# Opening of a fused attention and mixer kernel: first matmul tile by tile, one weight half on another queue, banks of premade queries by count

## Chip, cores, metric

The kernel runs on one core of a Trainium2 chip. The metric is the device time of one execution in microseconds (us); the time before is the median of three runs.

## The reference, cut

x is 2048 tokens by 512, in bf16. All that matters here:

```python
xn = layernorm(x)
q = (xn @ wq)                       # 32 heads of 128
s = softmax(q k^T / sqrt(128)) v    # 2048 cached keys and values per head
s = s @ wo
h = gelu(layernorm(xn) @ w1)        # 512 -> 512
hs = shift(h) @ w2                  # each quarter of the columns shifted by 1 or 2 tokens
x1 = xn + hs
b = x1 + gelu(layernorm(x1) @ w3) @ w4
out = x + s * silu(b)
```

For layernorm(xn), a normalised row normalised again, the kernel uses xn itself. The change concerns xn, xn @ w1 and the first few xn @ wq.

## The kernel before, in words

Tokens come in 16 tiles of 128. The work has three parts: an opening (L466 to L498 and the lines behind it) that makes xn, its transpose xnT, the mixer's first matmul and the first queries; the rest of the mixer and the MLP (m2, x1, ln2, m3, m4); and a long loop over 128 attention units (group of four heads, quarter of the tokens, head), which fills almost all of the time and keeps TensorE at work with scores, weighted values and output products.

Every instruction is pinned in program order, so each engine's order is the order in which the Python code emits it. An instruction that waits holds all that stand behind it on its engine, a DMA's issue among them: SyncE (nc.sync) and ScalarE (nc.scalar) issue loads as instructions of their own queues. DMA semaphores are reused, so a later load can wait, before it is issued, for the landing of an earlier one.

The steps of the opening, per tile t: `ln1_stats` (L189, VectorE: two statistics instructions; GpSimd: two small ones for the inverse root, L175 and L176), `ln1_norm` (L192, VectorE, writes xall), `tr_pe` (L195: four TensorE transposes into a bank of the pool psO, then ScalarE copies them to xnT, L199). `m1(c0, w)` (L204) multiplies w1 with w columns of xnT, in two steps of eight matmuls, each into a two-bank tile of psS, each followed by a gelu on ScalarE (L213) into hT. `m2` (L217) multiplies hT with w2, `x1` (L224) adds it to xall on VectorE. Tiles 8 to 15 are transposed by DMA (`tr_dma`, L201) from SyncE's queue. `q_ahead` (L509) makes one query block ahead of the loop: four matmuls of 512 columns into a bank of psX ("xa" or "xm", one buffer each), then a copy by ScalarE (L277). `tr_q` (L514) is a `q_ahead` and a `tr_pe`.

Before the change the opening loads x tiles 0 to 3 on both queues, both halves of w1 on SyncE (L468, L469), four wq blocks on ScalarE (L471), then a junk gelu (L472) that brings in the activation table. Twelve matmuls on zeros (L477) keep TensorE at work until the first transposes. The first four tiles go through in pairs: stats 0 and 1, norm 0, transposes 0, stats 2, norm 1, transposes 1, `m1(0, 256)`, stats 3, norm 2, transposes 2, norm 3, transposes 3, `m1(256, 256)`. Later blocks of four tiles use `ln1_block` (L498), which starts each block with the stats of its first tile. Queries are made ahead in four batches of four; the last batch (2 * HG, NU - 12, NU - 2, NU - 1) is numbers 8, 116, 126 and 127.

Of the kernel before, what the change touches and what calls it, by code (L numbers as in the profile page):

```python
# [8 lines left out]
ACT = mybir.ActivationFunctionType  # L9
ALU = mybir.AluOpType  # L10
FP32 = mybir.dt.float32
# [6 lines left out]
def kernel(  # L18
# [15 lines left out]
    nc = tc.nc  # L34
    P = nc.NUM_PARTITIONS
# [4 lines left out]
    _, H, Sk, Dh = A_k_cache.shape  # L40
# [3 lines left out]
    NT = Sq // P  # L44
    QT = Sq // 512
    DC = D // P
# [4 lines left out]
    HG = 4  # L51
# [6 lines left out]
    BASE_J = [3, 3, 2, 2]  # L58
# [3 lines left out]
    pin = tc.keep_in_program_order  # L62

    def pool(name, bufs=1, space=None, **kw):
        if space is not None:
            kw["space"] = space
        return tc.tile_pool(name=name, bufs=bufs, **kw)
# [3 lines left out]
    xnT = const.tile([P, DC, Sq], BF16, name="xnT")  # L71
# [11 lines left out]
    warm = const.tile([P, 512], BF16, name="warm")  # L83
# [9 lines left out]
    psX = ent(pool("psX", 1, PSUM))  # L93
    mid = ExitStack()
    psS = mid.enter_context(pool("psS", 2, PSUM, reuse_waits="tile"))
# [8 lines left out]
    w1_v = B_w1.rearrange("(dc p) j -> p dc j", p=P)  # L104
# [3 lines left out]
    def mm(out, lhsT, rhs, start, stop):  # L108
        pin(nc.tensor.matmul(out=out, lhsT=lhsT, rhs=rhs, start=start, stop=stop))  # L109
# [8 lines left out]
        out=ident[:], in0=diag[:], scalar1=0.0, scalar2=None, op0=ALU.is_equal))  # L118
# [34 lines left out]
    def load_w(h, eng=nc.sync):  # L153
        wqs[h] = wqp.tile([P, DC, Dh], BF16, name="wq_h")
        pin(eng.dma_start(out=wqs[h][:], in_=wq_v[:, :, h * Dh:(h + 1) * Dh]))
# [3 lines left out]
    def load_x(t, eng):  # L159
        xin[t] = tokp.tile([P, D], BF16, tag="ta", bufs=10, name="xin")  # L160
        pin(eng.dma_start(out=xin[t][:], in_=xsrc[t]))
# [3 lines left out]
    w1_sb = pL.tile([P, DC, D], BF16, name="w1_sb")  # L165
    w2_sb = pL.tile([P, DC, D], BF16, name="w2_sb")
    w3_sb = [pL.tile([P, DC, 2 * P], BF16, name=f"w3_sb{i}") for i in range(FC // 2)]
    hT = pL.tile([P, DC, Sq + PADW], BF16, name="hT")
# [9 lines left out]
    def stats(src, mv, rs, t):  # L178
        bn = smp.tile([P, nc.vector.BN_STATS_DIM], FP32, name="bn")
        pin(nc.vector.bn_stats(out=bn[:], in_=src))  # L180
        pin(nc.vector.bn_aggr(out=mv[:, t, :], in_=bn[:]))
        rsqrt(rs[:, t:t + 1], mv[:, t, 1:2])

    def norm_to(out, src, mv, rs, t):
        pin(nc.vector.tensor_scalar(
            out=out, in0=src, scalar1=mv[:, t, 0:1], scalar2=rs[:, t:t + 1],
            op0=ALU.subtract, op1=ALU.mult))

    def ln1_stats(t):  # L189
        stats(xin[t][:], mv1, rs1, t)  # L190

    def ln1_norm(t):  # L192
        norm_to(xall[:, t, :], xin.pop(t)[:], mv1, rs1, t)

    def tr_pe(t):  # L195
        tp = psO.tile([P, DC, P], FP32, tag="ps_o", name="ps_o")
        for dc in range(DC):
            mm(tp[:, dc, :], xall[:, t, dc * P:(dc + 1) * P], ident[:], True, True)
        pin(nc.scalar.activation(out=xnT[:, :, t * P:(t + 1) * P], in_=tp[:], func=ACT.Identity))  # L199
# [4 lines left out]
    def m1(c0, w):  # L204
        for jp in range(DC // 2):
            b = BASE_J[2 * jp]
            ps = psS.tile([P, 2, 512], FP32, name="ps_s")
            for j in range(2):
                jc = 2 * jp + j
                for dc in range(DC):  # L210
                    mm(ps[:, j, 0:w], w1_sb[:, dc, jc * P:(jc + 1) * P],
                       xnT[:, dc, c0:c0 + w], dc == 0, dc == DC - 1)
            pin(nc.scalar.activation(  # L213
                out=hT[:, 2 * jp:2 * jp + 2, b + c0:b + c0 + w], in_=ps[:, :, 0:w],
                func=ACT.Gelu_apprx_tanh))

    def m2(t):  # L217
        ps = psO.tile([P, D], FP32, tag="ps_o", name="ps_o")
        for jc in range(DC):
            c0 = BASE_J[jc] + t * P - SHIFT[jc]  # L220
            mm(ps[:], hT[:, jc, c0:c0 + P], w2_sb[:, jc, :], jc == 0, jc == DC - 1)
        return ps
# [41 lines left out]
    def q_mm(u, dcs, tag="xa"):  # L264
        g, qt, hh = units[u]
        if dcs[0] == 0:
            st[u] = dict(psq=psX.tile([P, 512], FP32, tag=tag, name="ps_q"))
        for dc in dcs:
            mm(st[u]["psq"][:], wqs[g * HG + hh][:, dc, :],
               xnT[:, dc, qt * 512:(qt + 1) * 512], dc == 0, dc == DC - 1)  # L270

    def q_copy(u, eng=None):
        qT = qtp.tile([P, 512], BF16, name="qT")
        if eng is None:
            pin(nc.vector.tensor_copy(out=qT[:], in_=st[u].pop("psq")[:]))  # L275
        else:
            pin(nc.scalar.activation(out=qT[:], in_=st[u].pop("psq")[:], func=ACT.Identity))  # L277
        st[u]["qT"] = qT
# [187 lines left out]
    for t, eng in enumerate([nc.sync, nc.scalar, nc.sync, nc.scalar]):  # L466
        load_x(t, eng)
    pin(nc.sync.dma_start(out=w1_sb[:, 0:2, :], in_=w1_v[:, 0:2, :]))  # L468
    pin(nc.sync.dma_start(out=w1_sb[:, 2:4, :], in_=w1_v[:, 2:4, :]))  # L469
    for h in range(HG):  # L470
        load_w(h, nc.scalar)  # L471
    pin(nc.scalar.activation(out=junk[:], in_=ones_t[:], func=ACT.Gelu_apprx_tanh))  # L472
    for t in range(4, 8):
        load_x(t, nc.sync)
    pin(nc.sync.dma_start(out=w2_sb[:], in_=w2_v))
    wps = psX.tile([P, 512], FP32, tag="xm", name="ps_warm")
    for _ in range(12):  # L477
        mm(wps[:], warm[:, 0:P], warm[:], True, True)
    for jc in range(DC):
        b = BASE_J[jc]  # L480
        pin(nc.gpsimd.memset(hT[:, jc, 0:b], 0.0))
        pin(nc.gpsimd.memset(hT[:, jc, b + Sq: Sq + PADW], 0.0))

    ln1_stats(0)
    ln1_stats(1)
    ln1_norm(0)
    tr_pe(0)
    ln1_stats(2)
    ln1_norm(1)
    tr_pe(1)  # L490
    m1(0, 256)
    ln1_stats(3)
    ln1_norm(2)
    tr_pe(2)
    ln1_norm(3)
    tr_pe(3)
    m1(256, 256)
    def ln1_block(ts, tr):  # L498
        ln1_stats(ts[0])
        for a, b in zip(ts, ts[1:]):  # L500
            ln1_stats(b)
            ln1_norm(a)
            tr(a)
        ln1_norm(ts[-1])
        tr(ts[-1])

    made = []

    def q_ahead(u):  # L509
        q_mm(u, range(DC), ("xa", "xm")[u % 2])  # L510
        q_copy(u, nc.scalar)
        made.append(u)

    def tr_q(t):  # L514
        q_ahead(t - 4)
        tr_pe(t)

    for t in range(8, 16):
        load_x(t, nc.sync)
    ln1_block(range(4, 8), tr_q)  # L520
    pend = [(t, m2(t)) for t in range(2)]
    ln1_block(range(8, 12), tr_dma)
    m1(512, 512)
    for t, ps in pend:
        x1(t, ps)
    for u in range(HG, 2 * HG):
        q_ahead(u)
    pend = [(t, m2(t)) for t in range(2, 4)]
    ln1_block(range(12, 16), tr_dma)
    for h in range((NG - 1) * HG, NG * HG):  # L530
        wqs[h] = pL.tile([P, DC, Dh], BF16, name=f"wq_e{h}")
        pin(nc.sync.dma_start(out=wqs[h][:], in_=wq_v[:, :, h * Dh:(h + 1) * Dh]))
# [7 lines left out]
    for u in range(NU - 4 * HG, NU - 3 * HG):  # L540
        q_ahead(u)
# [57 lines left out]
    for g in range(NG - 1):  # L599
        b = (g * QT + QT - 1) * HG  # L600
        for hh in range(HG):
            h = (g + 1) * HG + hh
# [81 lines left out]
    for n in range(UB * SPU):  # L684
        u, p = divmod(n, SPU)
# [42 lines left out]
    n = UB * SPU  # L728
# [23 lines left out]
    def bank(pl, tag, **kw):  # L752
        return pl.tile([P, D], FP32, tag=tag, name="ps_w", **kw)[:]

    ps = {0: bank(psX, "xm")}
# [81 lines left out]
```

## Time and profile before

| | us |
|---|---|
| runs | 1260.08, 1260.21, 1258.32 |
| median | 1260.08 |
| profiled execution, its time | 1261.13 |
| profiled execution, its span | 1259.4 |

The profile is of one execution. Its page gives the busy time of each engine (PE is TensorE, PEld its weight loads, DVE VectorE, ACT ScalarE, POOL GpSimd, SP SyncE), the chain of work that ended last, and groups of instructions. The trace answers further views: instructions in order of time (start, duration, engine, line, tiles, count, and in brackets the idle time before and what ended it), where ACTq and SPq stand for the queues that issue DMAs; the chain in order of time; busy times of stretches; and DMA rates of a stretch, by queue (q1 is SyncE's, q10 ScalarE's). A tile's name is shortened: w_sb is w1, w2, w3 or w4, told apart by the line.

### The profile page before, as it was taken

How to read it: one execution, taken by the hardware profiler on the slowest of the kernel's cores; microseconds unless marked ns; L12 is line 12 of the kernel's file. 1: busy time of each engine (PE TensorE's matmuls, PEld its weight loads, DVE VectorE, ACT ScalarE, POOL GpSimd, SP SyncE). 2: the span in 40 equal slices, each digit the busy share in tenths (PEclk: the TensorE clock that was granted, in tenths of full speed). 3: DMA queues.
4: the chain of work that ended last, by engine and by line, in shares of the span. 5: the costliest groups of instructions: out<-in, count | busy, mean ns of one | idle time of the engine just before them, and what ended most of it. 6: DMA issues, size and time to landing. Idle time of an engine off the chain costs nothing.

```text
span 1259.4 us, 16202 instructions
## 1 busy us (share of the span) xinstructions
PE 1239.5 (98%) x5782; PEld 598.3 (48%) x5899; DVE 1033.0 (82%) x1430; ACT 1100.7 (87%) x1113; POOL 34.4 (3%) x91
## 2 busy tenths in 40 slices
PE   8999999999999999999999999999999999999997
PEld 4444444444444444444444444444444444444443
DVE  7621567788888988888898988988898999988888
ACT  4344889999998999999999999999999999898886
POOL 4320000000000000000000000000000000000000
PEclk9999999999999999999999999999999999999999
DMA  6492012444345423454354524553364434452222
GB/s 155 106 169 72 10 30 46 82 91 93 60 72 97 110 58 76 88 110 84 47 101 94 104 50 76 96 116 69 55 101 102 101 66 82 92 97 54 68 56 59
DMA packets 224945, 103.86 MB, mean 82 GB/s; under 512 B 176928, under 2 KB 208160, under 8 KB 224864
## 3 DMA queue, kind: packets, MB, share of 16 engines
q1 hardware_dynamic: 221648, 100.07, 40.9%
q0 software_dynamic: 672, 1.84, 0.8%
q8 instruction: 46, 0.75, 0.3%
q10 hardware_dynamic: 2544, 0.92, 0.3%
q14 instruction: 35, 0.29, 0.1%
HBM read 67.90 MB, written 2.36 MB: 56 GB/s over the span
## 4 chain that ended last, share of the span: by engine, by line
PE 88%; DMA 5%; DVE 5%; ACT 1%; issue 1%; DVEq 0%; ACTq 0%; SPq 0%
PE ps_s L109 36%; PE ps_o L109 33%; PE ps_q L109 8%; PE ps_wo L109 8%; DMA rb<-dr 3%; PE ps_m L109 2%; DMA dr<-rc 2%; DVE oT L358 1%; DVE acc L302 1%; DVE sacc L411 1%; DVE sm L338 1%; DMA tT<-acc 0%; PE ps_warm L109 0%; ACT pT L291 0%; ACT xnT L199 0%
## 5 line engine op out<-in xcount | busy, mean ns | idle before, releaser
L291 ACT ACTIVATE pT<-ps_s 128x1024 bf16<-128x1024 f32 x1024 | 1034.6, 1023 | 79.1 <-PE ps_s L109 31.4
L109 PE MATMUL ps_s<-qT,kT 128*128 128x512 bf16 x2041 | 607.5, 379 | 0.6
L109 PE MATMUL ps_o<-pT,vb 128*128 128x512 bf16 x1962 | 588.9, 379 | 2.3 <-DVE oT L358 1.8
L302 DVE TENSOR_TENSOR acc<-acc,pT 128x2048 bf16<-128x2048 bf16 x255 | 309.2, 1213 | 73.4 <-ACT pT L291 68.6
L109 PEld LDWEIGHTS <-kT 128*128 128x128 bf16 x2048 | 231.0, 113 | 226.2 <-issue 0.8
L109 PEld LDWEIGHTS <-vb 128*128 128x128 bf16 x2048 | 200.2, 98 | 228.3 <-issue 3.0
L109 PE MATMUL ps_wo<-wo_h,oT 128*128 128x512 bf16 x492 | 177.8, 379 | 2.1
L109 PE MATMUL ps_q<-xnT,wq_h 128*128 128x512 bf16 x481 | 172.7, 379 | 2.1
L297 DVE TENSOR_TENSOR acc<-pT 128x2048 bf16<-128x2048 bf16 x128 | 155.7, 1216 | 6.1 <-ACT pT L291 5.9
L358 DVE TENSOR_TENSOR oT<-ps_o,rb 128x512 bf16<-128x512 f32 x127 | 124.4, 980 | 30.5 <-DMA rb<-dr 29.7
L307 DVE TENSOR_TENSOR acc<-acc 128x1024 bf16<-128x1024 bf16 x127 | 87.9, 692 | 4.3
L275 DVE CAST qT<-ps_q 128x512 bf16<-128x512 f32 x112 | 76.5, 683 | 0.3 <-PE ps_q L109 0.3
L109 PEld LDWEIGHTS <-oT 128*128 128x128 bf16 x508 | 48.5, 98 | 56.6 <-DVE oT L358 1.1
L109 PEld LDWEIGHTS <-wq_h 128*128 128x128 bf16 x484 | 47.2, 98 | 56.2 <-issue 0.2
L411 DVE TENSOR_TENSOR sacc<-ps_wo,sacc 128x512 f32<-128x512 f32 x96 | 65.5, 683 | 3.2 <-PE ps_wo L109 2.7
L338 DVE TENSOR_REDUCE sm<-tT 128x4 f32<-128x512 bf16 x96 | 64.7, 674 | 1.8 <-DMA tT<-acc 1.8
L308 DVE TENSOR_TENSOR acc<-acc 128x512 bf16<-128x512 bf16 x127 | 54.0, 425 | 4.3
L242 ACT ACTIVATE h2T<-ps_s 128x1024 bf16<-128x1024 f32 x28 | 28.6, 1023 | 24.1 <-PE ps_s L109 24.1
L109 PE MATMUL ps_s<-xn2T,w_sb 128*128 128x512 bf16 x219 | 48.6, 379 | 0.3
L109 PEld LDWEIGHTS <-w_sb 128*128 128x128 bf16 x304 | 29.7, 98 | 34.6 <-issue 2.1
L109 PEld LDWEIGHTS <-h2T 128*128 128x128 bf16 x224 | 21.5, 98 | 25.0 <-issue 0.2
L109 PE MATMUL ps_m<-w_sb,h2T 128*128 128x512 bf16 x106 | 31.0, 379 | 0.5
(73 smaller groups left out, 333.5 us busy)
## 6 DMA issues: line engine op xcount, KB each, us to landing
rb<-dr SPq DMA_DIRECT2D x127, 256.0 KB, 4.2
vb<-in_A_v_cache_dram SPq DMA_DIRECT2D x64, 256.0 KB, 3.3
wo_h<-in_A_wo_dram SPq DMA_DIRECT2D x32, 128.0 KB, 3.6
wq_h<-in_A_wq_dram SPq DMA_DIRECT2D x28, 128.0 KB, 3.3
w_sb<-in_B_w_dram SPq DMA_DIRECT2D x9, 256.0 KB, 5.0
kT<-in_A_k_cache_dram SPq DMA_TRANSPOSE x128, 3.3
xl<-in_A_x_dram SPq DMA_DIRECT2D x16, 128.0 KB, 3.7
dr<-rc SPq DMA_DIRECT2D x127, 2.0 KB, 1.4
```

The lines of the kernel that those rows point to most:

```text
L109: pin(nc.tensor.matmul(out=out, lhsT=lhsT, rhs=rhs, start=start, stop=stop))
L242: pin(nc.scalar.activation(out=h2[c, f][:], in_=ps[:], func=ACT.Gelu_apprx_tanh))
L275: pin(nc.vector.tensor_copy(out=qT[:], in_=st[u].pop("psq")[:]))
L291: pin(nc.scalar.activation(out=s["pT"][-1][:, jj:jj + 2, :], in_=sps[:], func=ACT.Exp, scale=SCALE))
L297: pin(nc.vector.tensor_tensor(out=s["acc"][:], in0=s["pT"][0][:], in1=s["pT"][1][:], op=ALU.add))
L302: pin(nc.vector.tensor_tensor(out=a[:], in0=a[:], in1=st[u]["pT"][i][:], op=ALU.add))
L307: pin(nc.vector.tensor_tensor(out=a[:, 0:2, :], in0=a[:, 0:2, :], in1=a[:, 2:4, :], op=ALU.add))
L308: pin(nc.vector.tensor_tensor(out=a[:, 0, :], in0=a[:, 0, :], in1=a[:, 1, :], op=ALU.add))
L338: pin(nc.vector.tensor_reduce(out=sm[:], in_=s["tT"][:], axis=mybir.AxisListType.X, op=ALU.add))
L358: pin(nc.vector.tensor_tensor(out=to, in0=o, in1=rb, op=ALU.mult))
L411: pin(nc.vector.tensor_tensor(out=sa, in0=ps[:], in1=sa, op=ALU.add))
```

## The change

Loads: the second half of w1 goes to ScalarE's queue ahead of the wq blocks; the fourth wq block goes to SyncE's queue, behind x tiles 4 to 7 and ahead of w2. Warm matmuls: eleven ahead of the first transposes, one between those of tiles 0 and 1. Statistics: always one tile ahead of the norm, across blocks as well (`ln1` takes the place of `ln1_block`). First matmul of tiles 0 to 3: one tile at a time, 16 matmuls of 128 columns into a one-bank tile (two in psX, two in psS), between the transposes of later tiles; its gelus are two per tile, of 128x256. In ScalarE's order the copies of transposes 0, 1 and 2 come ahead of the gelus of tile 0. Banks: a premade query takes "xa" or "xm" by how many were made before it, not by its number.

```diff
-    pin(nc.sync.dma_start(out=w1_sb[:, 2:4, :], in_=w1_v[:, 2:4, :]))
-    for h in range(HG):
+    pin(nc.scalar.dma_start(out=w1_sb[:, 2:4, :], in_=w1_v[:, 2:4, :]))
+    for h in range(HG - 1):
         load_w(h, nc.scalar)
...
     for t in range(4, 8):
         load_x(t, nc.sync)
+    load_w(HG - 1)
...
-    for _ in range(12):
-        mm(wps[:], warm[:, 0:P], warm[:], True, True)
+    def warm_mm(n):
+        for _ in range(n):
+            mm(wps[:], warm[:, 0:P], warm[:], True, True)
+
+    warm_mm(11)
...
+    def ln1(t, tr):
+        if t + 1 < NT:
+            ln1_stats(t + 1)
+        ln1_norm(t)
+        tr(t)
+
+    def m1_tile(t, pl, tag):
+        ps = pl.tile([P, DC, P], FP32, tag=tag, name="ps_m1")
+        for jc in range(DC):
+            for dc in range(DC):
+                mm(ps[:, jc, :], w1_sb[:, dc, jc * P:(jc + 1) * P],
+                   xnT[:, dc, t * P:(t + 1) * P], dc == 0, dc == DC - 1)
+        return ps
+
+    def gelu_tile(t, ps):
+        for jp in range(DC // 2):
+            b = BASE_J[2 * jp] + t * P
+            pin(nc.scalar.activation(
+                out=hT[:, 2 * jp:2 * jp + 2, b:b + P], in_=ps[:, 2 * jp:2 * jp + 2, :],
+                func=ACT.Gelu_apprx_tanh))
+
     ln1_stats(0)
-    ln1_stats(1)
-    ln1_norm(0)
-    tr_pe(0)
-    ln1_stats(2)
-    ln1_norm(1)
-    tr_pe(1)
-    m1(0, 256)
-    ln1_stats(3)
-    ln1_norm(2)
-    tr_pe(2)
-    ln1_norm(3)
-    tr_pe(3)
-    m1(256, 256)
-    def ln1_block(ts, tr):
...
+    ln1(0, tr_pe)
+    warm_mm(1)
+    ln1(1, tr_pe)
+    pm = [m1_tile(0, psX, "xa")]
+    ln1(2, tr_pe)
+    gelu_tile(0, pm[0])
+    pm.append(m1_tile(1, psX, "xm"))
+    ln1(3, tr_pe)
+    gelu_tile(1, pm[1])
+    for t in (2, 3):
+        gelu_tile(t, m1_tile(t, psS, "ps_s"))
...
-        q_mm(u, range(DC), ("xa", "xm")[u % 2])
+        q_mm(u, range(DC), ("xa", "xm")[len(made) % 2])
...
-    ln1_block(range(4, 8), tr_q)
+    for t in range(4, 8):
+        ln1(t, tr_q)
...
-    ln1_block(range(8, 12), tr_dma)
+    for t in range(8, 12):
+        ln1(t, tr_dma)
...
-    ln1_block(range(12, 16), tr_dma)
+    for t in range(12, 16):
+        ln1(t, tr_dma)
```

More of the change, by code (lines that the diff above doesn't have):

```diff
@@ L482 @@
         pin(nc.gpsimd.memset(hT[:, jc, b + Sq: Sq + PADW], 0.0))
-    ln1_stats(0)
-    ln1_stats(1)
-    ln1_norm(0)
-    tr_pe(0)
-    ln1_stats(2)
-    ln1_norm(1)
-    tr_pe(1)
-    m1(0, 256)
-    ln1_stats(3)
-    ln1_norm(2)
-    tr_pe(2)
-    ln1_norm(3)
-    tr_pe(3)
-    m1(256, 256)
-    def ln1_block(ts, tr):
[L499 to L505, printed above, removed]
+    def ln1(t, tr):
[16 more added lines that the diff above has]
+                func=ACT.Gelu_apprx_tanh))
+    ln1_stats(0)
+    ln1(0, tr_pe)
[9 more added lines that the diff above has]
+        gelu_tile(t, m1_tile(t, psS, "ps_s"))
     made = []
     def q_ahead(u):
-        q_mm(u, range(DC), ("xa", "xm")[u % 2])
+        q_mm(u, range(DC), ("xa", "xm")[len(made) % 2])
         q_copy(u, nc.scalar)
```

## The prediction

> **What bounds the kernel now.** I read the page first: span, busy times, the chain that ended last.
>
> ```profile
> span 1259.4 us, 16202 instructions
> PE 1239.5 (98%) x5782; PEld 598.3 (48%) x5899; DVE 1033.0 (82%) x1430; ACT 1100.7 (87%) x1113; POOL 34.4 (3%) x91
> PE 88%; DMA 5%; DVE 5%; ACT 1%; issue 1%; DVEq 0%; ACTq 0%; SPq 0%
> ```
>
> TensorE is busy for 1239.5 of 1259.4 us, and no other engine is as full. So only the 20 us in which it stands still, and any matmul time that is added, can move the end. The profiled execution took 1261.13 us, 1.73 us more than its span; the median of the three runs is 1260.08, about 1.05 us below it. I work out a difference against the profiled span and subtract it from the median. 0.2% is 2.5 us here, about what a measurement can tell from no change.
>
> The view by stretches tells where TensorE stands still in the part that the diff touches. The columns are us in the stretch, then busy us of each engine.
>
> ```profile
> 8.00:14.00 6.00, 4.59 (x42) 3.90 (x43) 4.73 (x13) 3.21 (x7) 3.56 (x10) 1.00 1.03 295
> 20.00:45.00 25.00, 24.76 (x113) 11.04 (x115) 15.99 (x35) 10.81 (x14) 6.69 (x17) 1.00 0.64 148
> 45.00:51.00 6.00, 4.63 (x22) 1.94 (x21) 3.85 (x10) 2.29 (x4) 3.08 (x8) 1.00 0.29 25
> ```
>
> There are two holes: 1.4 us between 8 and 14, and 1.4 us between 45 and 51. Between them it is busy for 24.76 of 25 us, so time won in the first hole is carried through. The chain of waits, in order of time, says what the first hole is made of.
>
> ```profile
> 6.94 1.15 ACT xnT L199 x2
> 8.14 1.92 PE ps_s L109 x16
> 10.08 0.60 ACT hT L213
> 10.68 0.98 ACT xnT L199 x2
> 11.71 1.91 PE ps_s L109 x16
> ...
> 14.52 0.60 ACT qT L277
> 15.11 0.49 ACT xnT L199
> ```
>
> ScalarE copies two transposed tiles, TensorE multiplies the two, ScalarE has a gelu and two copies to do, TensorE waits. From 14.52 on ScalarE alternates query copies and tile copies without a gap, 0.60 + 0.49 us a turn, until the last xnT. So the opening's result is read off at one point: when does the first query copy start, 14.52 now?
>
> **The change, part by part. 1. The queues.** The second half of w1 goes from SyncE's queue to ScalarE's, ahead of the wq loads, and the fourth wq load goes to SyncE's. In the changed kernel's instruction order this leaves a wait that the old one doesn't have: the third wq load, issued by ScalarE, now waits for the first half of w1 to land (the semaphore it reuses). Before, the third and the fourth waited for xin tiles 1 and 3. Behind that load in ScalarE's own queue stand the table load, the junk gelu and every xnT copy. When does that half land?
>
> ```profile
> 1.64 0.43 SPq L468 DMA_DIRECT2D w_sb<-in_B_w_dram  x1
> 4.42 0.37 ACTq L155 DMA_DIRECT2D wq_h<-in_A_wq_dram  x1
> 4.82 1.28 ACT L472 ACT_TABLE_LOAD   x1 [4.82 <-DMA xin<-in_A_x_dram]
> 6.12 0.20 ACT L472 ACTIVATE junk<-ones_t 128x1 bf16<-128x1 bf16 x1
> 6.45 0.33 SPq L161 DMA_DIRECT2D xin<-in_A_x_dram  x1
> 8.24 0.43 SPq L475 DMA_DIRECT2D w_sb<-in_B_w_dram  x1
> ```
>
> The half is issued at 1.64. The 6.45 row is the load of xin tile 6, which in the old order waits for just this half: it lands at about 6.45, 4.8 us after its issue. From the release of the last ScalarE load (4.42) to the end of the junk gelu (6.32) are 1.90 us. So if the half lands at L, ScalarE is ready for the first xnT at R = L + 1.92, where before it was ready at 6.32 and waited for TensorE until 6.94. Does L stay at 6.45 when the other half shares the transfer engines from the start?
>
> ```profile
> DMA packets 1242, 0.63 MB, mean 286 GB/s; under 512 B 823, under 2 KB 1242, under 8 KB 1242
> q1 hardware_dynamic: 447, 0.43, 60.4%
> q10 hardware_dynamic: 795, 0.20, 40.1%
> DMA packets 792, 0.76 MB, mean 378 GB/s; under 512 B 54, under 2 KB 792, under 8 KB 792
> ```
>
> The first three rows are 4.2 to 6.4 us: 0.63 MB at 286 GB/s, with 823 packets under 512 B on it, those of wq. The last row is 10.6 to 12.6, where nearly all packets are larger: 378 GB/s. In the changed kernel both halves, 0.51 MB, follow the four x tiles, of which the last lands at 4.42 (ScalarE's release above). From 4.2 that is 1.8 us at the first rate and 1.4 at the second, so the data is there at 5.6 to 6.0, and something follows until the semaphore. From above, a landing as slow as the slowest row of this stretch (wq, 6.2 us after its issue) would give 7.85; from below, part of the first half has moved before 4.2, so 5.2. I take L = 6.2, near the row of the same transfer, and R = 8.12. On SyncE the fourth wq load now stands ahead of w2 and x tiles 8 to 15 and waits for the second half, which by the same rates lands at about L too. That is 2 us before w2 goes out now (8.24), so I cost this at nothing; if the cover were gone, w2 would be late for m2, after the four queries. [...]
>
> **2. Tiles one by one.** What does one tile's first matmul cost? No row has these 16 matmuls of 128 columns; the nearest are the transposes, which are the same size.
>
> ```profile
> 9.78 0.54 PEld L109 LDWEIGHTS <-xall 128*128 128x128 bf16 x8
> 9.88 0.61 PE L109 MATMUL ps_o<-ident,xall 128*128 128x128 bf16 x8
> L213 ACT ACTIVATE hT<-ps_s 128x512 bf16<-128x512 f32 x4 | 2.4, 599 | 2.8 <-PE ps_s L109 2.8
> L213 ACT ACTIVATE hT<-ps_s 128x1024 bf16<-128x1024 f32 x2 | 2.1, 1026 | 3.5 <-PE ps_s L109 3.5
> ```
>
> Eight weight loads take 0.54 us, the last of them 0.1, so a pair has 0.063 us and a tile 1.01. Four tiles are 4.04 us where the two calls of m1 now take 1.92 + 1.91 in the chain: 0.2 us more TensorE work, but in pieces that fit between the copies. The gelu of 128x256: the two rows give 0.43 us for 512 more columns, so 0.60 - 0.21 = 0.385, two per tile 0.77. Now the sum from R = 8.12, with 0.575 for an xnT copy (two in 1.15), 0.25 for four transposes, 0.2 until a result can be read and 0.04 from a copy to the matmul behind it:
> - xnT0 8.12 to 8.70, xnT1 to 9.27. TensorE: tile 0 8.74 to 9.75, transposes of tile 2 to 10.00, readable at 10.20.
> - ScalarE: xnT2 10.20 to 10.78, two gelus to 11.57. TensorE meanwhile: tile 1 10.00 to 11.01, transposes of tile 3 to 11.26.
> - ScalarE: xnT3 11.57 to 12.15, gelus of tile 1 to 12.92. TensorE: tile 2 11.26 to 12.27, tile 3 12.27 to 13.28, the first query 13.28 to 14.14, readable at 14.34.
> - ScalarE: gelus of tile 2 to 13.69, of tile 3 to 14.46, then the first query copy: 14.46 instead of 14.52.
>
> So the opening wins 0.06 us: the pieces overlap well, and the later start of ScalarE, 8.12 against 6.94, takes it back. In general the gain is 6.26 - L: -1.6 at 7.85, +1.06 at 5.2. Is VectorE in the way, with the statistics of the next tile ahead of each norm?
>
> ```profile
> 7.72 0.41 DVE L185 TENSOR_SCALAR xall<-xin,mv,rs 128x512 bf16<-128x512 bf16 x1
> 8.90 0.41 DVE L185 TENSOR_SCALAR xall<-xin,mv,rs 128x512 bf16<-128x512 bf16 x1 [0.77 <-POOL rs L176]
> ```
>
> The norms of tiles 2 and 3 stand at 7.72 and 8.90; the new order puts the statistics of tile 4 into the 0.77 us that the second one waits for GpSimd anyway, so it stays there, and the transposes want it only at 11.01: 1.7 us of cover, at the price of whatever is missing should xin tile 4 land after 9.7. It is issued earlier than now. The later norms come some 1 us earlier, as their statistics no longer wait for a new block; TensorE uses none of that, because ScalarE's turns set its pace there. One warm matmul fewer ahead of the first transposes costs nothing, since these wait for the norm of tile 0, and it comes back between the transposes of tiles 0 and 1, where TensorE waits for the next norm; ScalarE, ready only at R, hides it all, at 0.43 us if it did not.
>
> **3. The banks.** The last four premade queries are numbers 8, 116, 126 and 127; by parity the first three share one bank, by count they alternate.
>
> ```profile
> 23.23 3.65 PE L109 MATMUL ps_q<-xnT,wq_h 128*128 128x512 bf16 x16
> 26.71 0.59 PE L109 MATMUL ps_o<-w_sb,hT 128*128 128x512 bf16 x2
> 45.15 1.03 PE L109 MATMUL ps_q<-xnT,wq_h 128*128 128x512 bf16 x4
> 46.87 1.02 PE L109 MATMUL ps_q<-xnT,wq_e 128*128 128x512 bf16 x4 [0.69 <-ACT qT L277]
> 48.58 1.89 PE L109 MATMUL ps_q<-xnT,wq_e 128*128 128x512 bf16 x8 [0.69 <-ACT qT L277]
> 50.30 0.59 PE L109 MATMUL ps_o<-w_sb,hT 128*128 128x512 bf16 x2
> ```
>
> A batch that alternates holds TensorE from 23.23 to 26.71, 3.48 us; this one from 45.15 to 50.30, 5.15. The edit is worth 1.67 us, on the path, as both stalls wait for a copy. What is late next? Behind it come five m2, whose sums VectorE adds, and then the first m3, which needs four transposes by DMA.
>
> ```profile
> 40.27 3.82 SPq L233 DMA_TRANSPOSE xn2T<-xn  x3
> 44.18 1.22 SPq L233 DMA_TRANSPOSE xn2T<-xn  x1
> DMA to landing us min/median/max: 2.4/2.4/4.1
> 54.77 1.46 PE L109 MATMUL ps_s<-xn2T,w_sb 128*128 128x512 bf16 x6
> ```
>
> The last is issued at 44.18 and lands by 48.3; m3 would come at 53.1: 4.8 us of cover. Everything after is ordered by waits on TensorE's work, so it moves along.
>
> **Sum:** 1.67 + 0.06 = 1.73 us; 1260.08 - 1.73 = 1258.3 us.
>
> **Rivals.**
> - **ScalarE is released early.** Without the small packets in between, L is 5.4 or less. The rate of 378 GB/s speaks for it; against it, the same half took until 6.45 with only 0.20 MB of wq beside it. The opening wins up to 1.06, the whole 2.5 to 2.7: 1257.2 to 1257.6. Chance 0.19.
> - **The small matmuls run slower than the transposes, or ScalarE is held up some more,** and the opening loses 0.5 to 1.6 us: 1258.9 to 1260.0. This needs L above 6.8, or a pair that takes over 0.075 us. Chance 0.18. [...]
> - **Slower: the held load.** ScalarE stands before its table load until w1's first half lands, and with it every copy of the opening. The whole change breaks even where 6.26 - L eats 1.67, at L = 7.93; the slowest row, 7.85, just misses that. At L = 9 it would be 1261.1. Chance 0.05.
> - **The banks do not pay,** because the copies' engine or VectorE holds the queue behind them: the copies take 0.60 us of each 0.87 us matmul group in the batch at 23.23 too, and no stall shows there. Only the opening's part is left: about 1260.0. Chance 0.03.
>
> **How the numbers follow.** My forecast, 1258.0 to 1258.9, has 0.55. Left out at the ends are about one in ten each side: the range is 1257.2 to 1260.0, the bounds of L. Faster by over 0.2% needs 2.5 us, so it has the first rival's 0.19 and a little of the forecast's upper end: 0.2. Slower by over 0.2% needs L above 10.4: 0.03. The rest, 0.77, is within.
>
> **What would show it.** The third wq load in ScalarE's queue should start at about 6.2, the table load at 6.6, the first xnT copy at 8.1 (6.94 now); TensorE should have no wait over 0.3 us between tile 0 and the first query copy at 14.4 to 14.5; the last four queries should take 3.5 us with no wait on a copy. I am wrong if the table load still starts before 5.5, if 16 small matmuls take 1.3 us, or if the m2 behind the queries wait for VectorE.

## The result and the profile after

| us | before | after |
|---|---|---|
| median (17 executions each) | 1260.06 | 1257.75 |
| lowest to highest | 1258.32 to 1262.11 | 1255.98 to 1258.86 |
| profiled execution, time | 1261.13 | 1256.22 |
| profiled execution, span | 1259.4 | 1254.4 |

The ratio is 0.9981, with a 95% interval of 0.9975 to 0.9987: 2.31 us less, where 1.73 were forecast. The predicted number is nearly the measured one. The parts of the sum are not, as the profile shows first and the experiments then.

Three lines of the page of the kernel after: span, busy times, the chain that ended last by engine.

```profile
span 1254.4 us, 16268 instructions
...
PE 1237.3 (99%) x5814; PEld 598.7 (48%) x5931; DVE 1031.8 (82%) x1430; ACT 1100.4 (88%) x1117; POOL 35.3 (3%) x91
...
PE 96%; DVE 2%; DMA 1%; issue 1%; ACT 1%; SPq 0%; DVEq 0%; ACTq 0%
```

TensorE still bounds the kernel. It has 64 instructions more (32 matmuls, 32 weight loads), and the chain runs through it for 96% of the span instead of 88%. The same stretches as before, in the kernel after:

```profile
8.00:14.00 6.00, 4.22 (x73) 4.12 (x73) 4.78 (x14) 5.03 (x13) 4.49 (x10) 1.00 1.00 296
20.00:45.00 25.00, 24.76 (x114) 11.17 (x115) 14.42 (x32) 10.71 (x14) 6.34 (x15) 1.00 0.62 143
45.00:51.00 6.00, 6.00 (x29) 2.69 (x28) 5.01 (x12) 2.39 (x4) 3.08 (x8) 1.00 0.11 22
```

The hole between 45 and 51 is gone: 6.00 busy of 6.00, 4.63 before. The hole between 8 and 14 has grown: TensorE is busy for 4.22 us there, 4.59 before. The chain of the kernel after, in order of time, says why.

```profile
1.65 5.67 DMA w_sb<-in_B_w_dram
7.32 0.02 issue
7.34 2.40 DMA wq_h<-in_A_wq_dram
9.74 0.04 issue
9.78 1.05 PE ps_m L109 x16
10.83 0.22 PE ps_o L109 x4
11.06 0.89 PE ps_m L109 x16
...
14.86 0.60 ACT qT L277
```

The opening now begins with a load of w1 that lands at 7.32, and what it releases is not a matmul but another load, the third of wq, in ScalarE's queue. The chain puts TensorE's wait until 9.78 on that wq load, but the rows speak for ScalarE's copy of tile 0: the copies start at 9.15, two take 1.07 us, and in a second profile of the same kernel (e9 below) the row of this matmul names the copy. From 9.78 on TensorE has no gap worth naming. Rows in order of time (start, duration, engine, line, tiles, idle time before and its cause) show both ends of that, and the two later places to read:

```profile
2.13 5.58 ACTq L155 DMA_DIRECT2D wq_h<-in_A_wq_dram  x3
7.75 1.28 ACT L472 ACT_TABLE_LOAD   x1 [7.75 <-DMA wq_h<-in_A_wq_dram]
9.15 1.07 ACT L199 ACTIVATE xnT<-ps_o 128x512 bf16<-128x512 f32 x2
9.78 1.05 PE L109 MATMUL ps_m<-xnT,w_sb 128*128 128x128 bf16 x16 [2.31 <-DMA wq_h<-in_A_wq_dram]
10.67 0.39 PE L109 MATMUL ps_o<-ident,xall 128*128 128x128 bf16 x4
12.70 1.95 ACT L506 ACTIVATE hT<-ps_m 128x256 bf16<-128x256 f32 x6
14.86 0.60 ACT L277 ACTIVATE qT<-ps_q 128x512 bf16<-128x512 f32 x1 [0.20 <-PE ps_q L109]
45.38 1.03 PE L109 MATMUL ps_q<-xnT,wq_h 128*128 128x512 bf16 x4
48.83 4.63 PE L109 MATMUL ps_o<-w_sb,hT 128*128 128x512 bf16 x20
127.12 1.28 ACT L291 ACT_TABLE_LOAD   x1
```

The third wq load leaves ScalarE's queue at 7.34, the table load starts at 7.75, the first copy at 9.15 and the first query copy at 14.86, where before it was 14.52: **the opening loses 0.34 us** in this execution. The last four queries take 48.83 - 45.38 = 3.45 us. The last row is a mark that serves all that follows: ScalarE loads the table of the loop's exponentials once. In the profile of before the same row reads

```profile
128.59 1.28 ACT L291 ACT_TABLE_LOAD   x1
```

so at the mark the changed kernel is 1.47 us ahead (1.67 - 0.34, and 0.14 from smaller things between). The spans differ by 5.0. What lies behind the mark, the loop, which the change does not touch, must be shorter too: 1259.4 - 128.59 = 1130.8 us before, 1254.4 - 127.12 = 1127.3 after. These three questions went to the chip: what does the held load cost, what are the banks worth, and why is the loop shorter?

### The profile page after: what moved, and what is told of

Same layout as the page of the kernel before. It is cut to its first block, busy times and chain, and to the rows that moved or that the text cites. A ratio compares the mean times of both kernels' runs of the same rounds, so it can differ in the third digit from the quotient of the medians.

```text
span 1254.4 us, 16268 instructions
## 1 busy us (share of the span) xinstructions
PE 1237.3 (99%) x5814; PEld 598.7 (48%) x5931; DVE 1031.8 (82%) x1430; ACT 1100.4 (88%) x1117; POOL 35.3 (3%) x91
## 3 DMA queue, kind: packets, MB, share of 16 engines
q10 hardware_dynamic: 2288, 1.05, 0.3%
## 4 chain that ended last, share of the span: by engine, by line
PE 96%; DVE 2%; DMA 1%; issue 1%; ACT 1%; SPq 0%; DVEq 0%; ACTq 0%
PE ps_s L109 39%; PE ps_o L109 36%; PE ps_q L109 9%; PE ps_wo L109 9%; PE ps_m L109 2%; DMA w_sb<-in_B_w_dram 0%; DVE acc L302 0%; DMA rb<-dr 0%; PE ps_sum L109 0%; PE ps_w L109 0%; DMA wq_h<-in_A_wq_dram 0%; ACT qT L277 0%; DVE y L392 0%; DVE xall L420 0%; ACT pT L291 0%
```

## The experiments

The theory on the opening: the banks win 1.67 us, and the third wq load, held in ScalarE's queue until w1's first half has landed, takes back what the tile-by-tile matmuls win. Its rival: the small pieces themselves are slow, and the hold is hidden. On the loop there were two theories: it is shorter because it starts earlier against transfers that don't move with it, or because the number of TensorE instructions ahead of it has changed. On the spread of the timed executions of after: the landing of w1 differs from one execution to the next.

Kernels marked [1], [2], [3] ran in three groups, each group beside its own runs of before on one chip (medians 1258.98, 1258.75 and 1259.34). "Mark" is the table load above; "rest" is the span less the mark. Both come from one profile of each kernel, the median and the ratio from its timed executions. The expectations' "first exp" stands 1.3 us behind the mark. The diffs are against the kernel that the text names.

| kernel | instructions | median | ratio to before, 95% | mark | rest |
|---|---|---|---|---|---|
| before, first profile | 16202 | | | 128.59 | 1130.8 |
| e1 before again [1] | 16202 | 1259.10 | 0.9999 (0.9990 to 1.0008) | 128.53 | 1129.1 |
| e2 banks alone [1] | 16202 | 1257.92 | 0.9990 (0.9981 to 0.9999) | 126.92 | 1129.0 |
| e8 loads alone [2] | 16202 | 1263.22 | 1.0034 (1.0021 to 1.0046) | 129.49 | 1129.3 |
| e11 loads alone, no hold [3] | 16202 | 1258.65 | 0.9998 (0.9989 to 1.0006) | 128.41 | 1129.2 |
| after, first profile | 16268 | | | 127.12 | 1127.3 |
| e9 after again [3] | 16268 | 1258.25 | 0.9988 (0.9979 to 0.9997) | 129.91 | 1127.4 |
| e6 after, old banks [2] | 16268 | 1260.03 | 1.0007 (0.9998 to 1.0015) | 127.97 | 1127.1 |
| e3 after, no hold [1] | 16268 | 1254.63 | 0.9963 (0.9950 to 0.9977) | 125.13 | 1127.1 |
| e10 the same again [3] | 16268 | 1254.26 | 0.9962 (0.9949 to 0.9976) | 125.33 | 1127.2 |
| e4 after, old loads [1] | 16268 | 1254.74 | 0.9966 (0.9954 to 0.9979) | 125.71 | 1127.2 |
| e5 banks, 64 more TensorE instructions [2] | 16266 | 1255.68 | 0.9975 (0.9966 to 0.9984) | 127.05 | 1127.0 |
| e7 no hold, 64 more [2] | 16332 | 1255.59 | 0.9970 (0.9960 to 0.9981) | 128.39 | 1127.2 |
| e12 w1 ahead of all wq [3] | 16270 | 1253.68 | 0.9959 (0.9946 to 0.9971) | 124.63 | 1127.1 |

### e1: before once more, without an edit

> The kernel before, unchanged, profiled a second time. Theory A (the change moves everything behind the opening by the same 1.47 us; what the two profiles differ by beyond that is stalls of single executions): the first exp of the loop at 129.9 us again, but the 2.3 us that the first profile lost around 380 to 416 us and the 0.8 us around 1075 to 1108 are not all there, or lie elsewhere; span between 1255.5 and 1259.5. Rival C (the earlier start makes the loop itself meet fewer late broadcasts): both losses at the same places again, span 1259 to 1260.

Its loop takes 1129.1 us, 1.7 less than in the first profile of before. So that much of the difference between the two first profiles (1130.8 against 1127.3) belonged to one execution: in the first profile the exponentials fall back between 380 and 416 us, here they don't. Some 1.8 us of the shorter loop remain to be explained. One profile of a kernel is not a sample of it.

### e2: the banks alone, in before

```diff
-        q_mm(u, range(DC), ("xa", "xm")[u % 2])
+        q_mm(u, range(DC), ("xa", "xm")[len(made) % 2])
```

> The kernel before with the banks alternating by count, nothing else. Theory A: last four premade queries in 3.5 us instead of 5.15, first exp of the loop 1.67 us earlier (128.2), time 1258.4 us, thus at least as fast as the whole change in the opening and TensorE part. Rival C: as the loop starts even earlier than in the whole change, 1257.5 us or less. Rival D (the copies or VectorE behind the batch hold the queue): less than 1 us earlier at the first exp.

The mark moves from 128.59 to 126.92, by 1.67 us; against e1 it is 1.61. The time falls by 1.06 us, with an interval of 0.1 to 2.4. The banks pay what the forecast said, up to the mark, and nothing behind it: the rest stays at 1129.0, as in e1.

### e3 and e10: after, with the held load taken off ScalarE

```diff
-    for h in range(HG - 1):
+    for h in range(HG - 2):
         load_w(h, nc.scalar)
...
+    load_w(HG - 2)
     load_w(HG - 1)
```

> The changed kernel with the third wq load issued from SyncE's queue too, so that nothing in ScalarE's queue ahead of the table load waits for w1. Theory A (the held load sets the start of the first tile): table load near 4.2 us instead of 7.75, first tile's matmul when w1's second half has landed, 7.6 to 8.0 instead of 9.78, first query copy at 13.0 (14.86 in the changed kernel), first exp of the loop 1.7 to 1.9 us earlier than in the changed kernel (126.6); time 1255.9. Rival E (w1's landing or the chain of copies and gelus sets the pace anyway): first query copy later than 14.3, time as the changed kernel's, 1257.7.

Rows of e3 in order of time:

```profile
3.92 1.28 ACT L472 ACT_TABLE_LOAD   x1 [3.92 <-DMA xin<-in_A_x_dram]
7.63 1.21 PE L109 MATMUL ps_m<-xnT,w_sb 128*128 128x128 bf16 x16 [0.41 <-DMA w_sb<-in_B_w_dram]
12.87 0.60 ACT L277 ACTIVATE qT<-ps_q 128x512 bf16<-128x512 f32 x1 [0.20 <-PE ps_q L109]
```

ScalarE has its table 3.8 us sooner, the first tile waits 0.41 us for w1 itself and for nothing else, and the first query copy comes at 12.87 instead of 14.86: the hold costs 1.99 us by the profiles. Tile by tile without it, the opening gains 14.52 - 12.87 = 1.65 us on before. The kernel is 4.35 us faster than before, and 1.3 us below the time expected; most of that is the difference between the two series of before (1260.06, and 1258.98 beside e3). e10 ran the same kernel beside e9, the changed kernel, on one chip:

> The changed kernel with the third wq load on SyncE, a second time, on the same chip as the changed kernel itself. Theory A: first query copy at 12.9, 2 us before the first profile of the changed kernel; time 2 to 3 us below the changed kernel of this call, about 1254.6, with a narrower spread. Rival E: no more than 0.5 us below.

1254.26 against 1258.25: there the hold costs 4.0 us, where 2 to 3 were expected, and twice what the profiles of after and e3 show. e9 explains the difference.

### e4: after, with the loads as they were before

```diff
-    pin(nc.scalar.dma_start(out=w1_sb[:, 2:4, :], in_=w1_v[:, 2:4, :]))
-    for h in range(HG - 1):
+    pin(nc.sync.dma_start(out=w1_sb[:, 2:4, :], in_=w1_v[:, 2:4, :]))
+    for h in range(HG):
         load_w(h, nc.scalar)
...
-    load_w(HG - 1)
```

> The changed kernel with the loads of before (both halves of w1 from SyncE, all four wq blocks from ScalarE); tile by tile, statistics ahead, warm matmuls and banks as changed. Theory A: table load at 4.8 as before, first tile's matmul when w1's second half has landed (7.6 to 7.9), first query copy at 13.0 to 13.2, first exp at 126.6 to 126.9; time 1255.9 to 1256.2: the two moved loads cost about 1.7 us and the tile by tile part gains 1.4 over the kernel before. Rival E: first query copy at 14.3 or later, time 1257.5 to 1258.

Rows of e4 in order of time:

```profile
4.65 1.28 ACT L472 ACT_TABLE_LOAD   x1 [4.65 <-DMA xin<-in_A_x_dram]
8.19 0.96 PE L109 MATMUL ps_m<-xnT,w_sb 128*128 128x128 bf16 x14 [0.75 <-DMA w_sb<-in_B_w_dram]
13.44 0.60 ACT L277 ACTIVATE qT<-ps_q 128x512 bf16<-128x512 f32 x1 [0.20 <-PE ps_q L109]
```

The opening is a little slower than expected (first query copy 13.44, 13.0 to 13.2 said) and the time over 1 us shorter (1254.74, 1255.9 to 1256.2 said), again about the difference between the series of before. No hold, so no late ScalarE; two matmuls of the first tile go out and the other 14 wait 0.75 us for the second half of w1. The mark is 0.58 us later than in e3, the times are the same (1254.74 and 1254.63). The loads of before would have served the tile-by-tile opening better than the loads of the change: 0.9966 against 0.9981 and, in e9, 0.9988 is 2 to 3 us.

### e8 and e11: the moved loads alone, in before, with and without the hold

e8 has the change's three load edits and nothing else of it. e11 differs from e8 in this:

```diff
-    for h in range(HG - 1):
+    for h in range(HG - 2):
         load_w(h, nc.scalar)
...
+    load_w(HG - 2)
     load_w(HG - 1)
```

> The kernel before with the two moved loads alone (second half of w1 to ScalarE's queue, fourth wq block to SyncE's), in pairs of tiles as before. Theory A: table load near 7.7 instead of 4.8, ScalarE ready near 9.2, both copies done near 10.3, first matmul of the pair at 10.3 instead of 8.14, first query copy 2.2 us later (16.7), first exp at 132.0, time 1261.2. Rival E (something else sets the opening's start): first query copy at 14.5 to 15.5, 1259.0 to 1260.

> The kernel before with w1's second half on ScalarE's queue as in the run with the two loads alone, but the third wq load on SyncE too. Only the held load differs from that run (1263.2). Theory A: table load near 4 us, first matmul of the pair at 8.1 or when w1 has landed (7.6), first query copy at 14.5, first exp at 129.9, time 1258.7 to 1259.3, as before: the hold alone costs 4 us there. Rival I (w1 on two queues lands late by itself): first query copy after 15.5, 1261 or more.

The table load of ScalarE, first in e8, then in e11:

```profile
6.63 1.28 ACT L472 ACT_TABLE_LOAD   x1 [6.63 <-DMA w_sb<-in_B_w_dram]
```

```profile
3.80 1.28 ACT L472 ACT_TABLE_LOAD   x1 [3.80 <-DMA xin<-in_A_x_dram]
```

Alone, the moved loads make the kernel slower by 4.3 us (interval 2.6 to 5.8); with the third wq load off ScalarE's queue nothing is left of that (0.9998). So the harm is the held load, not the half of w1 on the other queue, and the hold is not hidden. The numbers of e8's expectation were missed all the same. In its profile w1's first half landed at 6.20, over 1 us sooner than in after, so the table load came at 6.63 (7.7 said), the first query copy at 15.53 (16.7 said) and the mark only 0.9 us later than before; and the median is 2 us above the time said. The profiled execution took 1260.58 us, and the other four lie 2.3 us or more above it. e9 tells why. e11 came out as theory A said (first query copy at 14.46), but for a time 0.05 us below its range.

### e9: after once more

> The changed kernel, unchanged, profiled and timed a second time. Theory G (what spreads its times, and those of the other kernels with the held load, is when w1's first half lands): the third wq load leaves ScalarE's queue at another time than 7.34, the first query copy stands 7.5 us behind it as before (14.86 - 7.34), fetches and slow landings of the loop at the same places as in its first profile; time 1256 to 1259. Rival H (the loop spreads the times): same opening to 0.2 us, other stalls in the loop.

The time is that of the first series (1258.25, and 1257.75 there). The profile is not: the mark stands at 129.91, 2.79 us later. Stretches of e9 (the column behind the five engines is the granted TensorE clock):

```profile
6.00:9.00 3.00, 0.64 (x6) 0.32 (x5) 2.62 (x9) 1.01 (x1) 1.78 (x5) 0.93 0.77 222
9.00:12.00 3.00, 1.97 (x19) 1.97 (x19) 2.93 (x9) 1.45 (x4) 2.24 (x6) 0.50 1.00 243
12.00:15.00 3.00, 3.00 (x31) 3.00 (x30) 1.98 (x7) 1.66 (x5) 1.51 (x4) 0.50 1.03 341
15.00:20.00 5.00, 4.95 (x51) 3.52 (x51) 4.63 (x13) 4.31 (x12) 3.88 (x10) 0.96 0.29 57
```

and two rows of e9 in order of time:

```profile
7.99 1.28 ACT L472 ACT_TABLE_LOAD   x1 [7.99 <-DMA wq_h<-in_A_wq_dram]
...
10.03 1.86 PE L109 MATMUL ps_m<-xnT,w_sb 128*128 128x128 bf16 x16 [2.88 <-ACT xnT L199]
```

The hold ends 0.24 us later than in the first profile (7.99 against 7.75). That is a small part of the 2.79, so theory G doesn't explain this difference (the first query copy stands 10.05 us behind the release, not 7.5), and rival H, which wanted the same opening, fails too. The rest is the clock: from 9 to 15 us TensorE is granted 0.50, and 16 matmuls take 1.86 us where the first profile has 1.05 at a clock of 1.00. In steps of 0.2 us the view has the clock at 0.50 from 8.55 to 15.38. TensorE has work for 5.35 us of that, from 10.03 on; at half speed 2.7 us of it come late, and nearly all of this reaches the mark.

The drop falls into the gap that the hold makes: TensorE is idle from 7.15 to 10.03, 2.88 us, and the clock goes down 1.40 us after the gap begins. So the length of the gap alone does not decide: gaps of 2.31 us (the first profile of after) and 2.00 us (e8) brought no drop.

Two levels of the clock show here, 1.00 and 0.50, and the drop comes in one of two profiles of the same kernel. What sets it off and what ends it is not shown.

Is this the usual case? Each timed execution lists its mean granted clock. Of the 28 timed executions of the changed kernel (first series and e9) five have 0.999 or 1.000 and take 1254.81 to 1256.28 us; 23 have 0.996 to 0.998 and take 1257.10 to 1259.47. There is no overlap. e6 and e8, which hold the load too, divide in the same way: e6 at 0.999 and above 1256.88 and 1257.75, the other nine 1258.98 to 1261.19; e8 at 0.999 1260.58, the other four 1262.90 to 1263.94. e3, e10 and e12, which don't hold it, have 0.999 or 1.000 in all 15. So the first profile of after and the profiles of e6 and e8 show the minority of executions, the ones in which the clock stayed up. The others are slower by 1.8 us in the median in the first series of after, and by 2.7 (e6), 3.0 (e8) and 3.5 (e9); this comes on top of the price of the hold that those profiles show. That only the hold brings a lower clock is not so: one execution of e4 in 5 and one of e7 in 8 have 0.997. The mean doesn't say where in an execution the clock was low; e9 is the only profile that shows the drop in the opening.

### e6: after with the old banks

```diff
-        q_mm(u, range(DC), ("xa", "xm")[len(made) % 2])
+        q_mm(u, range(DC), ("xa", "xm")[u % 2])
```

> The changed kernel with the banks by parity again, that is the opening's part alone. Theory A with F: first query copy at 14.86 as in the changed kernel, the last four queries in 5.15 us again, first exp 0.2 us later than before (130.1), but without the 0.8 to 1.0 us near 1085; time 1258.3 to 1258.9, within 0.1% of before. Rival C: since the loop starts later than before, no gain in the loop, 1259.3 to 1260.

Missed: 1260.03. The profile misses on the other side: its execution took 1256.88 us, with the clock at 1.00 in the opening, the first query copy at 14.00 instead of 14.86, and the mark 0.62 us ahead of before. Nine of the eleven timed executions have the lower clock. The last four queries take 5.14 us again, and there is no wait near 1085, as said. Without the banks the change is no gain: 1.0007.

The opening of e6 is that of the changed kernel up to the first queries, and yet 0.86 us shorter in its profile. The cause is the landing of w1's first half: it comes at 6.46 in e6 and 6.20 in e8, at 7.32 in the first profile of after and 7.57 in e9. From the first copy to the first query copy e6 takes 5.71 us, exactly as the first profile of after. So where w1 lands early, the opening gains 0.52 us on before, and where it lands late, it loses 0.34. Over all 14 profiles of this document that load takes 4.6 to 6.3 us to land; why it varies is not shown.

### e5 and e7: 64 more TensorE instructions, no other work

e5 is e2 with 44 small warm matmuls instead of 12 large ones, about the same columns in all, so that TensorE has as many instructions as in the changed kernel (two fewer in all engines together). e7 does the same to e3 (43 of 128 columns for 11 of 512).

```diff
-    for _ in range(12):
-        mm(wps[:], warm[:, 0:P], warm[:], True, True)
+    for _ in range(44):
+        mm(wps[:, 0:140], warm[:, 0:P], warm[:, 0:140], True, True)
```

> The kernel before with the banks by count, and 44 warm matmuls of 140 columns in place of 12 of 512: the same warm time, but 64 instructions more in TensorE's stream, as many as the whole change adds. Theory F (what the change wins beyond its 1.47 us comes from where in the loop TensorE's instructions are fetched: a fetch beside a late broadcast or transpose of sums makes it land over a us later): first exp at 128.2 as with the banks alone, slow transposes of sums (over 4.9 us) near 303, 441, 579 as in the changed kernel instead of 340, 617, 893, no wait of the row sums near 1085, and a time 0.8 us below that of the banks alone: 1257.1. Rival C (it is the earlier start of the loop): as the banks alone, 1257.9, with the wait near 1085.

> The changed kernel without the held load (third wq load on SyncE), and 43 warm matmuls of 128 columns in place of 11 of 512: about as long, 64 more instructions for TensorE, 128 more than before. Theory F: opening as without the hold (first query copy 12.9, first exp at 126.4), slow transposes of sums at other places in the group than both, and a time that can differ by up to 1 us either way from the 1254.6 of that kernel. Rival: the fetches have no part, 1254.6 with the same places of slow landings.

Waits of TensorE in the whole run (total us, times, longest), e2 and then e5:

```profile
PE ps_s L109 <- ACT xnT L199: 1.9, 2, 1.2
PE ps_warm L109 <- DVE nhalf L114: 1.2, 1, 1.2
PE ps_sum L109 <- DVE qT L275: 1.1, 1, 1.1
PE ps_w L109 <- DVE oT L358: 0.7, 1, 0.7
...
PE ps_w L109 <- ACT tb L458: 0.4, 1, 0.4
```

```profile
PE ps_s L109 <- ACT xnT L199: 1.9, 2, 1.2
PE ps_warm L109 <- DVE nhalf L114: 1.2, 1, 1.2
PE ps_o L109 <- DVE xall L185: 0.6, 1, 0.6
PE ps_w L109 <- ACT tb L458: 0.4, 1, 0.4
```

The marks are 126.92 and 127.05, the times 1257.92 and 1255.68: with the same opening, 64 instructions in the warm-up win about 2 us, all of it behind the mark. That is more than the 0.8 us that theory F said. Two waits are gone, the first of them as said: the sums of the softmax, near 1084 us, and the last output products, near 1246. Both were for VectorE. Of the slow transposes of sums that theory F named, those near 441 and 579 come as said, the one near 303 does not. In the table the rest is 1129.0 to 1129.3 in four profiles with 16202 instructions (the fifth, the first of before, has the loss near 400 us that e1 doesn't have) and 1127.0 to 1127.4 in the nine with more, whatever their opening, their banks or their loads: the loop's length goes with the number of TensorE instructions ahead of it and with nothing else that was varied. An earlier start is not the cause: e9 reaches the mark later than before and has the short loop all the same. e7 has 64 more than the changed kernel and wins nothing further behind the mark (1127.2). In its profile the mark is 3.26 us later than e3's, which was not expected; the profiled execution is the slowest of eight (1257.33, the others 1253.63 to 1256.51), so this is more than the kernel's usual price. Two rows name most of it:

```profile
17.79 0.40 PE L109 MATMUL ps_o<-ident,xall 128*128 128x128 bf16 x4 [1.34 <-DVE xall L185]
...
33.23 3.92 PE L109 MATMUL ps_q<-xnT,wq_e 128*128 128x512 bf16 x15 [1.20 <-DMA wq_e<-in_A_wq_dram]
```

The first is the statistics one tile ahead: the norm of tile 7 stands behind the statistics of tile 8, whose x landed late.

What could connect a count of instructions with VectorE? In every kernel the page's queue rows hold this one (46 packets, 0.75 MB):

```profile
q8 instruction: 46, 0.75, 0.3%
```

That is some 16 KB a packet (0.75 MB in 46), and in the kernel after one packet for about 255 of TensorE's 11,745 instructions (5814 and 5931). The page gives their time, 0.3%, as a share of the same 16 DMA engines as that of the kernel's own transfers, and they move with the number of TensorE's instructions: in e5, with 64 more, they come 8 to 9 us earlier than in e2. That they carry TensorE's instructions is the author's reading of this and of the queue's name. At one place a packet and a load can be seen together. The load rb that VectorE needs for the softmax goes out at 1028.8 in e2, and the DMA view of e2 from 1031 to 1035 has an instruction packet in it; the load takes

```profile
DMA to landing us min/median/max: 5.4/5.4/5.4
```

and VectorE waits 0.8 us for it. The same load goes out at 1028.9 in e5, no instruction packet falls into 1029.5 to 1033.5, and it takes

```profile
DMA to landing us min/median/max: 4.1/4.1/4.1
```

with no wait. The next packet of e2 falls between 1059 and 1060, and the load rb issued at 1056.6 takes 4.3 us to land with a wait of 1.6 us; in e5 that load meets no packet, takes 3.6 us, and VectorE waits 0.4. The other profiles divide in the same way at these two places. In e1, e2, e8 and e11 a packet falls into both loads, they take 5.3 to 5.7 and 4.3 to 5.0 us, and VectorE waits 0.6 to 1.0 and 1.6 to 2.4 us; in the nine with more instructions no packet falls into either, they take 3.9 to 4.4 and 3.2 to 3.6 us, and VectorE waits at most 0.4.

That the number of instructions makes the loop shorter is shown (e5 against e2, and the two groups of the table). That it does so by where these packets fall among VectorE's loads is argued from such coincidences, since no run moved a packet alone: other loads of e5 are hit at other places (rb at 1117.9 takes 5.0 us), and cost TensorE nothing there.

### e12: w1 ahead of every wq load

```diff
-    for h in range(HG - 1):
-        load_w(h, nc.scalar)
...
-    load_w(HG - 1)
+    for h in range(HG):
+        load_w(h)
...
-        if t + 1 < NT:
+        if t == 8:
+            ln1_stats(8)
+        if t + 1 < NT and t != 7:
             ln1_stats(t + 1)
```

> The changed kernel with nothing on ScalarE's queue behind w1's second half: all four wq loads on SyncE behind x tiles 4 to 7; and the statistics of tile 8 behind the norm of tile 7, so that no norm of a tile that TensorE transposes waits for a tile still to be loaded. Theory A: with no small packets beside it w1 lands at 6.0 to 6.8, first tile's matmul near 7.0 (behind the copy of tile 0), first query copy at 12.1 to 12.5, 0.4 to 0.8 us below the kernel without the hold: about 1254.0. Rival: the wq blocks now land too late for the first queries, and the time is that of the kernel without the hold or above, 1254.6 to 1256.

Rows of e12 in order of time:

```profile
2.13 1.28 ACT L470 ACT_TABLE_LOAD   x1 [2.13 <-issue]
7.19 1.14 PE L109 MATMUL ps_m<-xnT,w_sb 128*128 128x128 bf16 x16
12.36 0.60 ACT L277 ACTIVATE qT<-ps_q 128x512 bf16<-128x512 f32 x1 [0.20 <-PE ps_q L109]
```

ScalarE's queue holds no load that waits, the first tile hardly waits for w1 (its halves land at 7.1 and 7.4, later than the 6.0 to 6.8 said), and the statistics of tile 8 no longer stand ahead of the norm of tile 7. 1253.68 us: 5.7 below before and 4.6 below the changed kernel on the same chip. This version beats both kernels. Against e10, which lacks only these two edits, it wins 0.6 us; what each of the two wins was not measured.

## Why the prediction was right, and where its steps were not

- **The bound.** TensorE, as said: whatever moved the end did so through its idle time, or through its clock.
- **When ScalarE is released: L was taken from one profile, and it varies.** The forecast took L = 6.2, with bounds of 5.2 and 7.85. It was 7.32 in the first profile of after and 7.57 in e9, but 6.46 in e6 and 6.20 in e8: all within the bounds, and up to 1.4 us from the value taken. The mechanism was the forecast one (e3 and e11 take the wait away and the time with it; e8, the loads alone, brings it), and R followed: 9.15, where L + 1.92 gives 9.24. The row from which L was read has a spread of its own: in the four other profiles with the old loads (e1, e2, e4, e5) the same half takes 5.1 to 5.6 us instead of 4.8. From 4.2 to 7.4 us the kernel after moves

```profile
4.20:7.40 3.20, 2.03 (x14) 0.84 (x13) 2.90 (x9) 0.00 (x0) 2.10 (x6) 1.00 1.04 294
```

  294 GB/s, hardly more than the 286 from 4.2 to 6.4 before. Whether w1 moves faster over two queues than over one, the rates don't tell: from 4.2 to 6.4 us they are 250 to 286 GB/s in the profiles with the old loads (259 in e4) and 251 to 329 in those with the moved ones.
- **The tile's price: right, a little high.** Sixteen matmuls from 9.78 to the transposes at 10.67 are 0.89 us (1.01 forecast), 0.056 a pair; six gelus take 1.95 us, 0.325 each (0.385). So after R the opening took 14.86 - 9.15 = 5.71 us instead of 6.34, and this gave back 0.63 of the 1.03 that the release was late. With the landing of e6, R is 8.29, 0.17 late, and the same 0.63 leave a gain of 0.52. The rival that a pair takes over 0.075 us is refuted by the same rows.
- **The opening's gain, +0.06:** -0.34 in the profile of after, +0.52 in e6's, by where w1 landed, and -3.1 in e9's with the lower clock (first query copy at 17.64). This is the term that was mis-sized in the sum. No step of the prediction named the clock, though its own held-load rival made TensorE stand idle: the rival priced the idle time, not a clock of 0.50 such as e9 shows from that idle time on.
- **The banks, 1.67:** right, 1.67 at the mark (e2), and 3.45 us for the four queries where 3.48 were said. The rival that they don't pay is refuted.
- **"Everything after ... moves along": wrong.** The loop became 1.8 us shorter (1129.1 in e1, 1127.3 after). It goes with the 64 instructions that the tile-by-tile matmuls add (e5 against e2). The prediction counted these as 0.2 us of TensorE work.
- **The covers.** w2 goes out no later than before and cost nothing; the warm matmul cost nothing. The statistics ahead cost nothing in after; in the profile of e7 they cost 1.34 us, at tile 8, where the prediction had looked at tile 4.
- **The sum.** Forecast 0.06 + 1.67 = 1.73. Measured, 1.8 (loop) + 1.67 (banks) less what the opening loses; to give 2.31 in the median, the opening must lose some 1.2 us, between the -0.34 and the -3.1 of the two profiles (a rough balance, since it sets profiles against a median). The number came out right by luck: a loss that was priced too low and a gain that was not seen nearly cancel. The range held, but not for the reasons given.
- **The signs.** In the first profile of after, third wq load at 7.34 (6.2 said), table load 7.75 (6.6), first copy 9.15 (8.1), first query copy 14.86 (14.4 to 14.5); no wait over 0.3 us on TensorE in between, and 3.45 us for the queries, as said.

Open: by which loads the instruction packets reach the loop, since no run moved one such packet alone; what lowers the clock in one execution and not in another, since no run varied the idle time by itself; and why the landing of w1 varies.

## What to carry to other kernels

Before moving a DMA into the queue of an engine that also computes, look at what the loads behind it wait for: here one load held on a reused semaphore held the table load (6.63 us in e8, 3.80 without the hold in e11) and every activation behind it, and in e9 the clock fell to 0.50 during TensorE's wait, which cost some 2.7 us on top of it. Split the span at a mark behind the edit and compare both sides over several kernels, so that a gain in a part that was not edited is seen and not credited to the edit. Take a second profile, and the clock of the timed executions, before one profile is called the kernel's.

## What the runs showed of the hardware

- The granted clock fell to 0.50 from 8.55 to 15.38 us, beginning 1.40 us into a TensorE gap of 2.88 us, in one of two profiles of the same kernel; a gap of 2.31 us in the other brought none. By their mean clock, 23 of its 28 timed executions lost some.
- 64 more TensorE instructions in the warm-up, with the same end of the opening to 0.13 us, shortened an unchanged loop by 2.0 us (1129.0 to 1127.0).
- A transfer that fell together with a packet of the instruction queue, some 16 KB, took 5.4 us to land, the same one without it 4.1 (e2 and e5); at two places of the loop, 13 profiles divide in this way.
- The same 256 KB half of w1, issued at 1.64 us, landed 4.6 to 6.3 us later in the 14 profiles.
